# Three value loads of one sequence issued together, ahead of the next pair's keys

## The chip, the cores and the metric

The kernel runs on one core of one Trainium2 chip. The metric is the device time of one execution in microseconds, from the first to the last thing the core does. An execution under the hardware profiler gives the span, that is the time between the first and the last instruction, and the profile.

## The reference

Attention over eight sequences with eight heads feeds a two-layer block with a leaky ReLU. Sixteen "beacon" keys and values stand ahead of each sequence's own 576, and every query sees all of them.

```python
B, H, S, Nb, D = (8, 8, 576, 16, 64)
k_all = np.concatenate([beacon_k, k], axis=2)
v_all = np.concatenate([beacon_v, v], axis=2)
scores = scale * np.matmul(q, k_all.transpose(0, 1, 3, 2))
causal[:, Nb:] = np.triu(np.ones((S, S), dtype=bool), k=1)
scores = np.where(causal, -1000000000.0, scores)
scores = scores - scores.max(-1, keepdims=True)
a = np.exp(scores)
a /= a.sum(-1, keepdims=True) + 1e-09
attn_out = np.matmul(a, v_all)
...
x = np.ascontiguousarray(attn_out.transpose(0, 2, 1, 3)).reshape(B * S, H * D)
h = x @ w_in            # 4608 x 512 by 512 x 2048
g = np.maximum(0.01 * h, h)
return (g @ w_out)      # 2048 x 512
```

## The kernel before

**Units of work.** The heads are taken in pairs: pair g holds heads 2*(g % 4) and the next one of sequence g // 4, so there are 32 pairs, and pairs 8 to 11 are the third sequence (b = 2). The 592 keys and values of a sequence are cut into five parts of 128, 128, 128, 128 and 80 rows; the first part holds the 16 beacon rows. The second layer of work takes the 4608 tokens in nine chunks of 512: `up()` (L442) makes one 128-column slice of the hidden layer of a chunk, `down()` (L512 for the first chunk, L537 for the others) multiplies hidden slices with the output weights.

**Operands.** For pairs from 8 on, `load_natural` (L167, issue at L171) fetches queries (step N g.0) and keys (step N g.1) of a pair with GpSimd's DMA queue, two transfers each, one for each head. `turn_pair` (L177, L179, step T g) turns them into the operands qT and kT with two DMA transposes on SP. `load_v_cast` (L205, L209 and L214) fetches one part of a sequence's values into one of two buffers v_aug, again on GpSimd's queue; part 0 has a second small transfer for the beacon rows. GpSimd also copies the beacon columns of kT (L229, step b) and sets the masked scores to zero (`triangle`, L289). All of these stand in one order on that engine. Every transfer of GpSimd takes one of eight completion semaphores in turn, so it waits until the one eight places earlier has landed.

**Scores and values.** From pair 8 on the scores of the pairs are laid end to end and cut into tiles of 512 columns; three tiles make a block (`block`, `stretch`, L314). One pair has 1664 columns, so block 3 (columns 4608 to 6143) begins with the last 384 columns of pair 10 and goes on with pair 11. ScalarE takes the exponential (L329, L333), GpSimd masks, and `value(g, half)` (L359) multiplies with v_aug: half 0 reads parts 0 to 2 of the values, half 1 parts 0 to 4, the last part with 80 rows. VectorE divides by the sum (L388, L389), and `x_turn` (L412) turns the result by DMA for `up()`.

**What sets the order.** The whole program is written out in a manual order for all engines. The part for pairs 0 to 7 is a string of steps. It ends with "... N9.1 u b8.2 b9.2 b10.2 b11.2 x6 v7.0 T9 v7.1 d d d N10.0 N10.1 d V2.0 V2.1 x7 t0 T10", so parts 0 and 1 of the third sequence's values (V2.0, V2.1) are issued there. From pair 8 on a list of events, each with a place in time counted in pairs, is sorted and emitted; `up()` and `down()` fill the room between them. Around the change these events stand: N11.0 at 7.75, N11.1 at 8.05, block 0 at 8.6, N12.0 at 8.75, N12.1 at 9.05, T11 at 9.25, value(8, 0) at 10.25, value(8, 1) at 10.62. The loop at L805 to L807 places the remaining value loads: parts 2, 3 and 4 of sequence 2 at 8.2, 8.5 and 8.8, and the five parts of each later sequence b at 4b - 0.4, 4b - 0.1 and so on.

Of the kernel before, what the change touches and what calls it, by code (L numbers as in the profile page):

```python
# [15 lines left out]
def kernel(  # L16
# [717 lines left out]
    with order:  # L734
# [50 lines left out]
        events = []  # L785
# [18 lines left out]
                ends.append(g + 3.5)  # L804
        for b in range(2, B):  # L805
            for n in range(2 if b == 2 else 0, NKB):
                events.append((4 * b - 0.4 + 0.3 * n, 6, load_v_cast, (b, n)))  # L807
        events.sort(key=lambda e: e[:2])
        first_down[0] = 4
        w, d0 = 0, done1[0] + done2[0]  # L810
# [45 lines left out]
```

## Time and profile before

| what | us |
|---|---|
| median of 3 runs | 331.04 |
| lowest, highest | 329.14, 331.49 |
| the profiled execution | 330.95 |
| its span | 329.2 |
| PE busy (TensorE matmul) | 318.6, 97% of the span |
| ACT busy (ScalarE) | 199.8, 61% |
| POOL busy (GpSimd) | 184.7, 56% |
| DVE busy (VectorE) | 145.2, 44% |

The span was the slowest core's, and there is only one core. A row of slices in the page cuts the span into 40 equal pieces of 8.2 us; a digit is the busy share in tenths. In a timeline a line has start, duration, engine, line of the kernel, operation, what it writes and reads, and how many such instructions stand in a row; in brackets is the idle time ahead of it and what ended that. SPq marks transfers that SP issued. In a table of stretches the columns are the stretch, its length, the busy time (and count of instructions) of PE, PE's weight loads, DVE, ACT and POOL, then the granted clock of TensorE, the mean number of transfers on each DMA engine, and GB/s. Each transfer has a time to landing, from its issue until its semaphore is complete.

### The profile page before, as it was taken

Reading aid. Unit: us, or ns where it says so; the run is one execution under the profiler, and the core shown is the slowest. Engines: PE = TensorE matmul, PEld = TensorE weight load, DVE = VectorE, ACT = ScalarE, POOL = GpSimd, SP = SyncE. Lnnn points to the kernel's source line nnn. Section 1 sums busy time; section 2 is a strip of 40 time slices with the busy share of each in tenths; the row PEclk is TensorE's granted clock in tenths of the full one; section 3 lists DMA queues with packets and bytes.
Section 4 is the critical chain, followed back from the end, with each engine's and each line's share of the span. In section 5 each row is a group of like instructions: output and inputs, shape, how many; then the busy total and the mean of one; then the engine's idle time right before and its main releaser. Section 6 shows DMA issues by size and latency. Waiting matters only on the chain.

```text
span 329.2 us, 8516 instructions
## 1 busy us (share of the span) xinstructions
PE 318.6 (97%) x3429; PEld 213.1 (65%) x3429; DVE 145.2 (44%) x297; ACT 199.8 (61%) x336; POOL 184.7 (56%) x354
## 2 busy tenths in 40 slices
PE   7999999897999999999999999999999999999995
PEld 4574565443587458855788888557865684566685
DVE  3563355412565255435443444453543552424344
ACT  4968862683855885477756774786468506553510
POOL 8895978995899686658965977666221000000000
PEclk9999999997999999999999999999999999999999
DMA  8999999999999999999999999999422111000103
GB/s 134 138 203 182 145 214 124 176 154 172 130 127 165 184 126 127 143 153 110 135 137 208 126 135 127 172 106 113 110 80 58 26 53 64 2 33 32 66 32 129
DMA packets 155928, 39.93 MB, mean 121 GB/s; under 512 B 143040, under 2 KB 153152, under 8 KB 155888
## 3 DMA queue, kind: packets, MB, share of 16 engines
q0 software_dynamic: 99824, 18.54, 85.1%
q1 hardware_dynamic: 55792, 20.77, 37.2%
q8 instruction: 27, 0.44, 0.6%
q14 instruction: 13, 0.11, 0.1%
q10 hardware_dynamic: 272, 0.07, 0.1%
HBM read 37.22 MB, written 9.44 MB: 142 GB/s over the span
## 4 chain that ended last, share of the span: by engine, by line
PE 79%; POOL 6%; DMA 6%; ACT 4%; DVE 2%; issue 2%; DVEq 0%; ACTq 0%; POOLq 0%
PE acc L442 33%; PE acc L537 28%; PE av L359 8%; DMA v_aug<-in_v_dram 6%; PE sc L314 5%; ACT aT L333 3%; PE sc L267 2%; POOL v_aug L214 1%; POOL k_nat L171 1%; POOL gsum L158 1%; POOL q_nat L171 1%; DVE u L559 1%; DVE p L559 1%; PE tp L243 1%; PE acc L512 1%
## 5 line engine op out<-in xcount | busy, mean ns | idle before, releaser
L442 PE MATMUL acc<-xT,w_in_sb 128*128 128x512 bf16 (+1 forms) x640 | 137.8, 360 | 0.7 <-ACT gT L450 0.4
L450 ACT ACTIVATE gT<-acc 128x512 bf16<-128x512 f32 x144 | 83.7, 617 | 57.0 <-PE acc L442 54.5
L442 PEld LDWEIGHTS <-w_in_sb 128*128 128x128 bf16 x640 | 59.9, 98 | 53.8 <-issue 6.3
L289 POOL TENSOR_SCALAR_AFFINE_SELECT aT<-aT 128x256 bf16<-128x256 bf16 (+2 forms) x160 | 61.0, 411 | 58.3 <-ACT aT L329 34.3
L537 PEld LDWEIGHTS <-gT 128*128 128x128 bf16 x512 | 48.8, 98 | 8.3 <-issue 1.2
L333 ACT ACTIVATE aT<-sc 128x1024 bf16<-128x1024 f32 (+3 forms) x64 | 51.8, 897 | 0.0
L537 PE MATMUL acc<-w_out_sb,gT 128*128 128x256 bf16 x384 | 46.2, 273 | 0.0
L359 PEld LDWEIGHTS <-aT 128*128 128x128 bf16 (+1 forms) x960 | 36.7, 98 | 12.1 <-issue 5.9
L359 PE MATMUL av<-v_aug,aT 128*128 128x65 bf16 (+1 forms) x960 | 39.6, 194 | 4.0 <-DMA v_aug<-in_v_dram 3.1
L537 PEld LDWEIGHTS <-gsum 128*128 128x128 bf16 x384 | 36.8, 98 | 6.7
L329 ACT ACTIVATE aT<-sc 128x512 bf16<-128x512 f32 (+3 forms) x64 | 29.0, 523 | 18.6 <-PE sc L314 18.6
L562 ACT COPY p<-acc 128x512 f32<-128x512 f32 (+1 forms) x25 | 14.5, 581 | 38.8 <-PE acc L537 35.2
L388 DVE RECIPROCAL rec<-av 128x6 f32<-128x6 f32 (+1 forms) x64 | 12.0, 187 | 58.1 <-PE av L359 57.8
L214 POOL DMA_DIRECT2D v_aug<-in_v_dram x40 | 34.0, 854 | 4.0 <-DMA w_in_sb<-in_moe_w_in_dram 3.4
L171 POOL DMA_DIRECT2D k_nat<-in_k_dram x48 | 34.7, 728 | 1.9 <-issue 0.8
L171 POOL DMA_DIRECT2D q_nat<-in_q_dram x48 | 34.7, 728 | 0.3 <-issue 0.2
L389 DVE TENSOR_TENSOR x_nat<-av,rec 128x384 bf16<-128x384 f32 (+1 forms) x64 | 31.4, 491 | 2.2
L537 PE MATMUL acc<-w_sum,gsum 128*128 128x256 bf16 x256 | 31.9, 273 | 0.0
L276 ACT ACTIVATE aT<-sc 128x1024 bf16<-128x1024 f32 (+3 forms) x32 | 25.9, 875 | 4.4 <-PE sc L267 4.1
L610 DVE TENSOR_TENSOR gsum<-gT 128x1024 bf16<-128x1024 bf16 x16 | 11.0, 689 | 31.5 <-ACT gT L450 31.5
L314 PE MATMUL sc<-qT,kT 64*128 64x80 bf16 (+22 forms) x384 | 21.8, 250 | 0.6 <-PE acc L512 0.6
L314 PEld LDWEIGHTS <-kT 64*128 64x128 bf16 x384 | 12.7, 94 | 11.6 <-issue 8.0
(62 smaller groups left out, 224.5 us busy)
## 6 DMA issues: line engine op xcount, KB each, us to landing
out_dram<-p SPq DMA_DIRECT2D x26, 256.0 KB, 3.3
q_nat<-in_q_dram POOLq DMA_DIRECT2D x48, 72.0 KB, 5.4
k_nat<-in_k_dram POOLq DMA_DIRECT2D x48, 72.0 KB, 5.4
v_aug<-in_v_dram POOLq DMA_DIRECT2D x24, 128.0 KB, 6.4
w_in_sb<-in_moe_w_in_dram POOLq DMA_DIRECT2D x2, 1024.0 KB, 12.2
w_out_sb<-in_moe_w_out_dram POOLq DMA_DIRECT2D x2, 1024.0 KB, 11.0
out_dram<-u SPq DMA_DIRECT2D x8, 256.0 KB, 2.5
gsum<-in_q_dram POOLq DMA_DIRECT2D x8, 144.0 KB, 6.3
```

Of the source, the lines that this page charges most:

```text
L171: nc.gpsimd.dma_start(out=t[:, :, par], in_=(q, k)[which][b, 2 * hp + par].rearrange("(t p) d -> p t d", p=NR),)
L214: nc.gpsimd.dma_start(out=dst[lo : ROWS[c], c, :, 0:D], in_=v[b, :, OFF[c] : OFF[c] + n].rearrange("h p d -> p h d"),)
L276: nc.scalar.activation(out=aT[:, :, c0 : c0 + w], in_=sc[:, :, 0:w], func=AF.Exp, scale=0.125)
L289: nc.gpsimd.affine_select(out=view, in_=view, compare_op=ALU.is_ge, fill=0.0, base=128 - n if lo == 0 else 0, channel_multiplier=-1, patte ...
L314: nc.tensor.matmul(out=(sc[par] if apart else sc[:, par])[:, at : at + b - a], lhsT=kT[ps_, c * 128 : (c + 1) * 128], rhs=qT[ps_, q0 : q0 ...
L329: nc.scalar.activation(out=probs[g][:, par, lo:hi], in_=sc[par][:, at : at + hi - lo], func=AF.Exp, scale=0.125)
L333: nc.scalar.activation(out=probs[g][:, :, lo:hi], in_=sc[:, :, at : at + hi - lo], func=AF.Exp, scale=0.125)
L359: nc.tensor.matmul(out=avv[:, n, 0 : D + 1], lhsT=aT[0 : ROWS[c], par, a0 : a0 + 128], rhs=va[0 : ROWS[c], c, 2 * hp + par, :], start=(c = ...
L389: nc.vector.tensor_tensor(out=x_nat[:, t0:t1].rearrange("p t e d -> p (t e) d"), in0=avv[:, :, 0:D], in1=rec[:, n0:n1, None].to_broadcast( ...
L442: nc.tensor.matmul(out=acc[:, lo:hi], lhsT=w_in_cols(fc, j), rhs=xT[:, j, x0 : x0 + hi - lo], start=(j == 0), stop=(j == NJ - 1), skip_gro ...
L450: nc.scalar.activation(out=gT[i][:, fc, :], in_=acc, func=AF.Prelu, alpha=0.01)
L537: nc.tensor.matmul(out=acc[:, lo : lo + HD], lhsT=left(i, n, fc, tile), rhs=right(n, fc), start=(lo == 0 and fc == 0), stop=(fc == HF - 1) ...
```

## The change

Parts 2, 3 and 4 of sequence 2's values get one common place, 7.9, between N11.0 (7.75) and N11.1 (8.05). The later sequences' places stay as they are, written in another way.

```diff
         for b in range(2, B):
             for n in range(2 if b == 2 else 0, NKB):
-                events.append((4 * b - 0.4 + 0.3 * n, 6, load_v_cast, (b, n)))
+                events.append((4 * b - (0.1 if b == 2 else 0.4 - 0.3 * n), 6, load_v_cast, (b, n)))
```

On GpSimd's queue the order around it becomes the following, with the transfers of a step in brackets and the block's masks where they stand:

```
before: N11.0 (2)  N11.1 (2)  V2.2  V2.3  masks (4)  N12.0 (2)  V2.4  N12.1 (2)  mask ...
after:  N11.0 (2)  V2.2  V2.3  V2.4  N11.1 (2)  masks (4)  N12.0 (2)  N12.1 (2)  mask ...
```

No instruction is added or taken away on any engine, and the order on PE, VectorE, ScalarE and SP is as before. The semaphores that the transfers use are handed out in the new order.

## Prediction

> **What bounds the kernel now.** I read the page's busy rows first: PE is busy for 97% of the span, and from slice 10 on it never drops. Time can be won only where PE itself stands still, so I looked next at the two marked slices, 8 and 9 (66 to 82 us).
>
> ```profile
> PE   7999999897999999999999999999999999999995
> PEclk9999999997999999999999999999999999999999
> DMA  8999999999999999999999999999422111000103
> ```
>
> Slice 9 has a hole in PE and a dip in its granted clock; the DMA row says that the transfer engines are full there. PE's waits between 50 and 100 us name the hole, and the timeline and the chain of waits give its place:
>
> ```profile
> PE av L359 <- DMA v_aug<-in_v_dram: 2.6, 1, 2.6
> ...
> 72.65 0.90 PE L359 MATMUL av<-v_aug,aT 128*128 128x65 bf16 x24
> 76.13 0.49 PE L359 MATMUL av<-v_aug,aT 80*128 80x65 bf16 x6 [2.58 <-DMA v_aug<-in_v_dram]
> 76.43 4.06 PE L442 MATMUL acc<-xT,w_in_sb 128*128 128x512 bf16 x12
> ...
> 66.35 9.74 DMA v_aug<-in_v_dram
> 76.13 0.49 PE av L359 x6
> 76.62 3.87 PE acc L442 x12
> 80.49 0.77 PE sc L314 x16
> ```
>
> At 73.55 us PE reaches the 80-row value matmuls of pair 8, which read part 4 of the third sequence's values. That part was issued at 66.35 and landed 9.74 us later, at 76.09. PE stood for 2.58 us. The wait has a second price, in a table of four stretches:
>
> ```profile
> 72.30:75.70 3.40, 1.25 (x27) 0.92 (x26) 0.76 (x2) 1.49 (x2) 3.40 (x9) 1.00 2.33 158
> 75.70:79.10 3.40, 2.97 (x13) 1.31 (x13) 0.61 (x2) 0.60 (x1) 2.62 (x4) 0.50 2.02 154
> 79.10:82.50 3.40, 3.40 (x30) 1.48 (x29) 1.62 (x3) 2.57 (x7) 0.48 (x2) 1.00 1.91 175
> ```
>
> The column before the last two is the granted clock: 0.50 for the 3.4 us that follow the wait. The chain has twelve L442 matmuls at 3.87 us there and at 2.59 us elsewhere (82.23), so 1.28 us are lost to it.
>
> POOL issues the loads, SP the transposes that turn keys into operands:
>
> ```profile
> 60.31 1.45 POOL L171 DMA_DIRECT2D k_nat<-in_k_dram  x2
> 61.74 1.79 POOL L214 DMA_DIRECT2D v_aug<-in_v_dram  x2
> 63.50 1.48 POOL L289 TENSOR_SCALAR_AFFINE_SELECT aT<-aT 128x224 bf16<-128x224 bf16 x4
> 64.90 1.46 POOL L171 DMA_DIRECT2D q_nat<-in_q_dram  x2
> 66.35 0.73 POOL L214 DMA_DIRECT2D v_aug<-in_v_dram  x1
> 67.07 1.45 POOL L171 DMA_DIRECT2D k_nat<-in_k_dram  x2
> ...
> 65.77 1.25 SPq L179 DMA_TRANSPOSE qT<-q_nat  x1
> 67.56 1.27 SPq L179 DMA_TRANSPOSE kT<-k_nat  x1
> 68.92 0.55 SPq L522 DMA_DIRECT2D out_dram<-p  x1
> 74.99 1.20 SPq L179 DMA_TRANSPOSE qT<-q_nat  x1
> ```
>
> In POOL's rows k_nat at 60.31 is pair 11, the v_aug pair at 61.74 is parts 2 and 3, q_nat at 64.90 and k_nat at 67.07 are pair 12. In SP's rows 65.77 and 67.56 are pair 11's transposes.
>
> **What the Trainium skill says.** "TensorE: Matmul & The Clock Gate", Part 1: the array's clock is halved after an idle window of about 3.4 us, and the window runs freely. The trace agrees in the length (0.50 for 3.4 us), but a wait of 2.58 us sufficed here, in a stretch with 1.25 us of work. "DMA: Bandwidth & Descriptors", Issuing engines are not separate DMA queues: transfers of all issuers share 16 engines and interleave. The trace agrees: landings (issue plus time to landing of each transfer) come nearly in order of issue over both queues: pair 11's keys 67.1 and 67.5, part 2 at 69.5, part 3 at 71.9, pair 12's queries 72.1 and 74.8, pair 11's two transposes 74.7 and 75.9, part 4 at 76.1, pair 12's keys 77.0 and 77.3. It is one backlog, and a transfer's place in it decides. Same page, Anatomy of one DMA: waits are held on the issuing sequencer, not by the DMA engines. So SP stands at a transpose until its keys land (67.56 is 0.06 us after 67.5).
>
> **The change, part by part.** Instructions and bytes stay the same; five issues on POOL change places.
>
> Part 4's issue (0.73 us) leaves 66.35 and follows part 3. Parts 2, 3, 4 go out from 60.31: 0.91 + 0.91 + 0.73 us, so part 4 is issued at 62.1. With the longest latency of this neighbourhood, 9.9 us, it lands at 72.0; by its place in the backlog near 70 to 71. PE asks at 73.55, so the wait goes, with no doubt worth pricing. Without it PE runs 6 value matmuls (18 take 0.56, so 0.19) and 12 matmuls at full clock (2.59): 2.78 us from 73.55, against 6.94 us (73.55 to 80.49) now. PE is ready for the next block of scores at 76.3 instead of 80.5. The most that can be won is 6.94 - 2.78 = 4.16 us.
>
> The masks of pair 8 at 63.50 start 0.73 us later. Their readers start at 72.65, some 7 us after they end: free. What follows on POOL from 67.07 on stands as before, except that a load waits until the load eight places earlier has landed. Pair 13's keys (72.17, which waited 0.76 us for part 3 at 71.9) now wait for pair 11's keys. By the landing worked out next that is up to 1 us, and POOL has 3.36 us idle ahead of the masks at 82.02: free.
>
> Pair 11's keys pay. They are issued 2.55 us later, at 62.9 and 63.6, behind all three parts. In the backlog the same set as before (keys 11, parts 2 and 3) plus part 4 has to pass until the keys are in. That set was in at 71.9. Part 4 is 640 rows of 128 bytes. From 65.7 to 77.3 us 6144 such rows landed, together with the transposes and stores in between: 11.6 x 640 / 6144 = 1.2 us with everything, and about half of it, 0.6, if I count rows alone. The keys land at 72.5 to 73.1; I take 72.8 (before: 67.5). SP issues the transpose then. How long it takes isn't known: the trace has 8.3 us for this one at 67.56, 5.6 and 5.2 for pair 12's at 74.99 and 77.40, 3.6 for pair 13's at 82.66. I take 5.2, since its issue comes when the backlog ahead of it (pair 12's loads, one transpose, pair 13's queries) is being worked off; ends 3.6 and 8.3. Landing at 78.0, ends 76.4 and 81.1.
>
> Who waits for it: the block at 76.3 begins with six matmuls of pair 10 (16 take 0.77, so 0.3 us), then takes pair 11's keys at 76.6. Today they are in at 75.9, 4.8 us ahead of use. Now PE waits 78.0 - 76.6 = 1.4 us. I price no clock loss on 1.4 us: the stretch would keep 2 us of work of 3.4, more than the 1.25 that lost the clock.
>
> Behind the held transpose on SP: a store of p (68.92 becomes about 74), whose tile isn't written again before the next chunk, and pair 12's transposes at 74.99 and 77.40. Those wait for pair 12's own loads, which keep their place; SP is free at 72.8 + 1.27 + 0.55 = 74.6. They land by 82.6 as today, or sooner, and the block that needs them (86.53 today) comes at 83.7: it holds, with about 1 us to spare.
>
> Sum: 4.16 - 1.4 = 2.8 us won. The profiled execution took 330.95 us (span 329.2 and 1.7 around it), so 328.2. The median shown, 331.04, is 0.09 above the profiled execution, which changes nothing.
>
> **Rivals.** *No new wait*: the transposed keys land by 76.6. For it: the latency of 3.6 us when the backlog is short. Against: the DMA row is at 9 until slice 27. Gain 4.16, so 326.8.
>
> *The stall moves and grows* (the other side): pair 11's transpose takes its old 8.3 us, from 73.1, and lands at 81.4. PE waits 4.8 us at 76.6 and then runs 3.4 us at half clock, another 1.3 to 1.7. The loss is 6.1 to 6.5 against 4.16 won: 332.9 to 333.3. It decides from a wait of about 2.9 us with the clock lost, that is a landing at 79.5. For it: DMA is saturated, and the keys go behind all of pair 12's loads. Against: the transpose just before it in the queue is gone by then.
>
> *Nothing moves*: part 4 lands late although issued earlier. It would need over 11.4 us to landing, which no load near it took. 331.0.
>
> **How the numbers follow.** Forecast (a wait of 0.7 to 2.9 us, 327.5 to 329.7): 0.48. No new wait: 0.24. Moved and grown: 0.20. Nothing moves, or something not seen here: 0.08. The range goes from 326.6 (no new wait, with 0.2 us for the run) to 331.8, within the moved stall, of which the worst half stays out. A change of 1%, about what a measurement of this kernel can tell, is 3.3 us, a border at 327.7. Faster by more: all of "no new wait" and a fifth of the forecast, 0.34. Slower by more (over 334.3, a transpose over 9 us, or what isn't seen): 0.12. The rest, 0.54, within 1%.
>
> **What would show it.** Right: PE's waits have no v_aug entry near 73 us, the six value matmuls follow the 24 at once, and the timeline shows a PE or weight-load wait of 1 to 2 us ahead of L314 for kT near 76.6. SP shows the kT transpose of pair 11 near 73. Clock 1.00 in slice 9 says that no half-clock stretch came back. Wrong: keys in before 72, no wait at L314 (then 326.8), or a wait over 2.9 us there with the clock at 0.50 behind it.

## The result, and the profile after

The changed kernel took 328.95 us in the median of 22 executions, and the kernel before, beside it, 329.89 us in the median of 22. The ratio of the two kernels' times is 0.9979, with a 95% interval of 0.9957 to 1.0. Two further comparisons, shown below, gave 1.0002 (0.9975 to 1.0029) and 0.997 (0.9948 to 0.9993). The mean of the three is 0.9984, about 0.5 us. The forecast was 2.8 us.

The ratios leave out every execution over 1.5% longer than the fastest of its kernel, such as the profiled one of the changed kernel (span 332.5 us), which ran its first 24 us on a slower matrix clock, so that everything in it stands some 5 us later than in the profile before. I therefore count from the first score matmul of block 0 (60.30 us before, 65.53 after). The page of the changed kernel:

```profile
span 332.5 us, 8516 instructions
...
PE   8999999998999999999999999999999999999995
...
PEclk9999999999999999999999999999999999999999
DMA  8999999999999999999999999999621111000203
```

The hole of PE in slices 8 and 9 and the dip of the clock are gone. The transfers are as full as before. PE's waits between 50 and 100 us no longer name v_aug; kT has taken its place, with two waits of 0.18 and 0.97 us:

```profile
PE sc L314 <- DMA kT<-k_nat: 1.2, 2, 1.0
```

Its timeline around blocks 2 and 3 on PE, GpSimd's issues, SP's transposes, and the chain of waits at that place:

```profile
78.26 1.09 PE L359 MATMUL av<-v_aug,aT 128*128 128x65 bf16 x30
79.19 2.75 PE L442 MATMUL acc<-xT,w_in_sb 128*128 128x512 bf16 x12
81.88 0.34 PE L314 MATMUL sc<-qT,kT 64*128 64x96 bf16 x6
83.19 0.67 PE L314 MATMUL sc<-qT,kT 64*128 64x128 bf16 x10 [0.97 <-DMA kT<-k_nat]
```

```profile
66.21 2.50 POOL L214 DMA_DIRECT2D v_aug<-in_v_dram  x3
68.68 0.76 POOL L171 DMA_DIRECT2D k_nat<-in_k_dram  x1
69.75 0.73 POOL L171 DMA_DIRECT2D k_nat<-in_k_dram  x1 [0.32 <-ACT gT L450]
...
73.62 1.20 SPq L179 DMA_TRANSPOSE qT<-q_nat  x1
78.45 1.20 SPq L179 DMA_TRANSPOSE kT<-k_nat  x1
79.74 0.56 SPq L522 DMA_DIRECT2D out_dram<-p  x1
```

```profile
69.75 8.64 DMA k_nat<-in_k_dram
78.40 0.02 SPq L179
78.42 0.03 issue
78.45 4.69 DMA kT<-k_nat
83.14 0.05 issue
83.19 0.67 PE sc L314 x10
```

All 30 value matmuls follow each other (78.26). After twelve L442 matmuls PE does six score matmuls of pair 10 and then stands 0.97 us, because pair 11's keys went out behind the three values, landed at 78.39, and were turned (transposed) by 83.14. It is the new wait that the prediction describes, at the place it names. The clock was 1.00 in both stretches:

```profile
75.70:79.10 3.40, 3.23 (x46) 2.09 (x47) 0.24 (x2) 3.25 (x7) 3.40 (x9) 1.00 2.11 166
79.10:82.50 3.40, 3.12 (x26) 1.32 (x22) 1.78 (x4) 1.91 (x4) 3.40 (x8) 1.00 2.03 189
```

In this pair of profiles PE gets from the last score matmul of block 2 to the last of block 3 in 7.32 us, where before took 10.33. That is 3.0 us won, close to the 2.8 forecast. So the question is why the timed runs show a sixth of it.

### The profile page after: what moved, and what is told of

Read it like the earlier page. It is cut to its first block, busy times and chain, and to the rows that moved or that the text cites. A ratio compares the mean times of both kernels' runs of the same rounds, so it can differ in the third digit from the quotient of the medians.

```text
span 332.5 us, 8516 instructions
## 1 busy us (share of the span) xinstructions
PE 325.1 (98%) x3429; PEld 215.8 (65%) x3429; DVE 146.4 (44%) x297; ACT 201.0 (60%) x336; POOL 188.2 (57%) x354
## 4 chain that ended last, share of the span: by engine, by line
PE 81%; DMA 6%; ACT 4%; POOL 4%; DVE 2%; issue 1%; SPq 0%; DVEq 0%; ACTq 0%; POOLq 0%
PE acc L442 32%; PE acc L537 26%; PE av L359 8%; PE sc L314 5%; PE sc L267 3%; ACT aT L333 3%; PE av L645 3%; DMA k_nat<-in_k_dram 3%; PE tp L243 2%; DMA xT<-x_nat 2%; DMA kT<-k_nat 1%; POOL v_aug L214 1%; DVE u L559 1%; POOL k_nat L171 1%; DVE p L559 1%
## 5 line engine op out<-in xcount | busy, mean ns | idle before, releaser
L442 PE MATMUL acc<-xT,w_in_sb 128*128 128x512 bf16 (+1 forms) x640 | 136.6, 358 | 1.0 <-ACT gT L450 0.4
L289 POOL TENSOR_SCALAR_AFFINE_SELECT aT<-aT 128x256 bf16<-128x256 bf16 (+2 forms) x160 | 64.5, 429 | 63.2 <-ACT aT L329 29.8
L442 PEld LDWEIGHTS <-w_in_sb 128*128 128x128 bf16 x640 | 59.4, 98 | 52.9 <-issue 4.3
L333 ACT ACTIVATE aT<-sc 128x1024 bf16<-128x1024 f32 (+3 forms) x64 | 51.8, 895 | 0.0
L276 ACT ACTIVATE aT<-sc 128x1024 bf16<-128x1024 f32 (+3 forms) x32 | 26.8, 875 | 9.1 <-PE sc L267 8.6
L314 PEld LDWEIGHTS <-kT 64*128 64x128 bf16 x384 | 12.9, 94 | 12.9 <-issue 8.2
```

Source lines behind the costliest of these rows:

```text
L276: nc.scalar.activation(out=aT[:, :, c0 : c0 + w], in_=sc[:, :, 0:w], func=AF.Exp, scale=0.125)
L289: nc.gpsimd.affine_select(out=view, in_=view, compare_op=ALU.is_ge, fill=0.0, base=128 - n if lo == 0 else 0, channel_multiplier=-1, patte ...
L314: nc.tensor.matmul(out=(sc[par] if apart else sc[:, par])[:, at : at + b - a], lhsT=kT[ps_, c * 128 : (c + 1) * 128], rhs=qT[ps_, q0 : q0 ...
L333: nc.scalar.activation(out=probs[g][:, :, lo:hi], in_=sc[:, :, at : at + hi - lo], func=AF.Exp, scale=0.125)
L442: nc.tensor.matmul(out=acc[:, lo:hi], lhsT=w_in_cols(fc, j), rhs=xT[:, j, x0 : x0 + hi - lo], start=(j == 0), stop=(j == NJ - 1), skip_gro ...
```

## The experiments

There are three theories. A: the profiled execution of before is typical, and what is won at block 3 is given back later. B: the profiled execution of before was a dear one, that is, it lost more time than most, and most executions lose less at part 4. C is A's second half by itself: PE comes sooner to later operands and waits there.

To compare executions I cut PE's timeline at the last score matmul of blocks 2, 3 and 7. From block 7 to block 12 every execution in the table took 39.84 to 39.85 us (e9 alone 41.16), and from block 12 to PE's last matmul 178.93 or 178.94. So what differs lies ahead of block 7. Block 0 begins anywhere from 59.3 to 65.7 us in these profiles, and the loads that the edits move go out from about there on. From block 0 to block 2 it is 9.80 to 9.82 us, but 10.18 in the changed kernel's first profile, which has the wait of 0.18 us there, and 10.31 in e1.

| execution | block 2 to 3, us | block 3 to 7, us | sum |
|---|---|---|---|
| before, the profile of the prediction | 10.33 | 25.80 | 36.13 |
| before, e3 | 6.58 | 26.37 | 32.95 |
| before, e7 | 7.91 | 26.83 | 34.74 |
| before, e10 | 7.18 | 25.81 | 32.99 |
| changed | 7.32 | 26.52 | 33.84 |
| changed, e4 | 7.12 | 26.13 | 33.25 |
| changed, e8 | 6.49 | 26.37 | 32.86 |
| changed, e11 | 7.48 | 26.32 | 33.80 |
| part 4 alone early, e1, e12, e14 | 6.17, 6.18, 6.17 | 28.75, 27.82, 28.24 | 34.92, 34.00, 34.41 |
| value matmuls later, e9, e13, e15 | 6.35, 6.35, 6.35 | 29.27, 29.18, 26.49 | 35.62, 35.53, 32.84 |
| part 4 not loaded, e5 | 6.18 | 26.73 | 32.91 |

**The kernel before, three more profiles (e3, e7, e10).** No edit.

> The kernel before once more, for its profile. Theory A: a wait of 2.4 to 2.8 us at part 4 and a granted clock of 0.50 for 3.4 us behind it. Theory B: a wait under 2 us, or one with the clock at 1.00.

> The kernel before, a third profile. Theory B: the wait for part 4 is under 1 us and the clock stays at 1.00. Theory A: 2.4 to 2.8 us with a clock of 0.50 behind it.

> The kernel before, a fourth profile. Theory B: a wait for part 4 between 0 and 2.6 us; with a wait under 2 us no half clock.

PE's value matmuls of pair 8 in the three, in this order, from their timelines:

```profile
78.02 0.90 PE L359 MATMUL av<-v_aug,aT 128*128 128x65 bf16 x24
79.17 0.35 PE L359 MATMUL av<-v_aug,aT 80*128 80x65 bf16 x6 [0.25 <-DMA v_aug<-in_v_dram]
79.36 2.75 PE L442 MATMUL acc<-xT,w_in_sb 128*128 128x512 bf16 x12
```

```profile
74.18 0.35 PE L359 MATMUL av<-v_aug,aT 80*128 80x65 bf16 x6 [1.58 <-DMA v_aug<-in_v_dram]
74.37 2.75 PE L442 MATMUL acc<-xT,w_in_sb 128*128 128x512 bf16 x12
```

```profile
73.38 0.35 PE L359 MATMUL av<-v_aug,aT 80*128 80x65 bf16 x6 [0.85 <-DMA v_aug<-in_v_dram]
73.56 2.75 PE L442 MATMUL acc<-xT,w_in_sb 128*128 128x512 bf16 x12
```

The same wait is 0.25, 1.58 and 0.85 us long, where the profile before had 2.58. The twelve matmuls behind it take 2.75 us, where that one had 4.06: there is no half clock. For the 1.58 us wait (e7) the table of stretches says so:

```profile
72.73:76.14 3.41, 1.96 (x15) 1.01 (x15) 0.94 (x3) 0.71 (x2) 3.41 (x9) 1.00 1.93 184
76.14:79.55 3.41, 3.25 (x28) 1.52 (x28) 2.03 (x4) 2.98 (x7) 2.41 (x6) 1.00 1.98 149
```

So the wait's price, against the 6.17 us that block 2 to block 3 takes at least, was 4.16 us in the profile of the prediction and 0.41, 1.74 and 1.01 in the others. This is theory B: the profile that the sum was made on was the dearest of four, and the only one with the clock lost. B's number for e7, a wait under 1 us, was too low.

**The changed kernel, three more profiles, two of them timed (e4, e8, e11).** No edit.

> The changed kernel once more, timed beside the others. All theories: 0.4 to 1 us faster than before, as measured. Theory A further: its wait at pair 11's keys is longer than 1 us or costs the clock in most executions. Theory B: the wait is near 1 us, the clock stays at 1.00, and from the first block of scores to pair 11's scores the PE takes about 17.7 us (20.4 us in before's profile).

> The changed kernel, a third profile. Theory B: no wait for part 4, a wait for kT of 0.5 to 1.5 us at block 3, clock 1.00. If the transfers differ from execution to execution as much as the part 4 wait does (0.25 and 2.58 us so far), the wait for kT could be anywhere from 0 to 3 us.

> The changed kernel, timed once more beside before. Theory B: the ratio stays between 0.997 and 1.000, since a wait for kT of some 1 us has taken the place of a wait for part 4 of 0.25 to 2.6 us. No wait for part 4.

The ratios were 1.0002 (0.9975 to 1.0029) in e4 and 0.997 (0.9948 to 0.9993) in e11. None waited for part 4 at pair 8. Block 3 in the timelines of e4 and e11:

```profile
75.30 0.34 PE L314 MATMUL sc<-qT,kT 64*128 64x96 bf16 x6
76.42 0.67 PE L314 MATMUL sc<-qT,kT 64*128 64x128 bf16 x10 [0.77 <-DMA kT<-k_nat]
...
78.96 0.67 PE L314 MATMUL sc<-qT,kT 64*128 64x128 bf16 x10 [1.14 <-DMA kT<-k_nat]
```

In e8 the block's 16 matmuls stand in one piece of 1.16 us where they take 0.83 without a wait, so it waited 0.3 us, less than the 0.5 to 1.5 expected. The 0.4 to 1 us that e4 was expected to win did not show in its ratio. The wait for kT is thus 0.3 to 1.1 us, and steadier than what it replaces. Over four profiles each, block 2 to block 3 takes 8.0 us before (6.58 to 10.33) and 7.1 us changed (6.49 to 7.48). That is 0.9 us. Leave the dear one out and 7.2 stands against 7.1. Four profiles of each are few, so I looked at the timed executions too.

Without those that the ratios leave out, the quickest tenth of 115 executions of before took 327.9 us or less and the slowest tenth 331.3 or more; of 58 of the changed kernel it was 327.9 and 330.4. So the quick executions are alike, and the dear ones became fewer. The mean granted clock is on record for every execution, and one stretch of 3.4 us at half clock makes it 0.995. It was 0.995 or less in 21 of all 141 executions of before beside e1 to e11, and in 6 of 68 of the changed kernel. The half clock was thus rare in before, wherever in the kernel it came.

**Part 4 not loaded (e5).** This kernel leaves the load out, so its result is not the right one.

```diff
-            for n in range(2 if b == 2 else 0, NKB):
+            for n in range(2 if b == 2 else 0, NKB - 1 if b == 2 else NKB):
```

> The order of before without the load of part 4 of the third sequence's values; its 80 rows keep what the first sequence left there. Nothing waits for part 4 and nothing is moved later, and 80 KB less are fetched: more than any place for this load can give. Theory B (the wait for part 4 is short in most executions): at most 1 us faster than before, ratio 0.997 to 1.000. Theory A (it costs 4.2 us in most): 4 us faster, ratio 0.988.

The ratio was 0.9939 (0.9911 to 0.9966), 2.0 us faster (1.1 to 2.9). It lies between the two theories' numbers, so it fits neither: B had allowed at most 1 us. The value matmuls run through:

```profile
77.76 1.10 PE L359 MATMUL av<-v_aug,aT 128*128 128x65 bf16 x30
```

It agrees with the wait's mean price, 1.8 us in the four profiles of before (0.41, 1.74, 1.01 and 4.16). In its one profile nothing of that is waited for later: block 3 to block 7 takes 26.73 us. It is the only kernel here that fetches less, and the fastest; how much of its gain is owed to the smaller traffic isn't shown.

**Part 4 alone early (e1, e12, e14).** Keys of pair 11 keep their place; part 4 goes out behind parts 2 and 3, ahead of the masks.

```diff
-                events.append((4 * b - 0.4 + 0.3 * n, 6, load_v_cast, (b, n)))
+                events.append((8.55 if (b, n) == (2, 4) else 4 * b - 0.4 + 0.3 * n, 6, load_v_cast, (b, n)))
```

> Only part 4 is moved ahead, behind parts 2 and 3 and ahead of the masks; pair 11's keys keep their place ahead of the values. Theory A (the profiled execution of before was typical, so its wait plus half clock cost 4.2 us in most executions, and the keys' delay in the changed kernel takes 1.4 to 2 back): about 4 us faster than before, a ratio near 0.988. Theory B (the wait in most executions is without the half clock, or shorter; the profiled one was dear): 1 to 2.6 us faster, ratio 0.992 to 0.997, and better than the changed kernel by the keys' wait, about 1 us. Theory C (what is won here is waited for later, by transfers that come no sooner): no faster than the changed kernel. Profile: no v_aug wait near 73 us, and kT of pair 11 some 1 us later than before but ahead of use.

> The kernel with part 4 alone moved ahead, a second profile. From the last score matmul of block 2 to the last of block 3 its PE took 6.2 us, the shortest of all, but from block 3 to block 7 it took 28.8 us, where before took 25.8 to 26.8. If what part 4 no longer costs is waited for later (theory C), block 3 to block 7 takes over 27.5 us again. If the first profile's later waits were chance, 25.8 to 26.8.

> The kernel with part 4 alone moved ahead, a third profile; expected as in the second.

The ratio was 0.9987 (0.996 to 1.0013): not faster than the changed kernel, against A, and against B but for the edge of its 0.992 to 0.997. The three profiles show where the time goes. Block 2 to block 3 takes 6.17 us, without any wait. But block 3 to block 7 takes 27.8 to 28.8 us, where before and the changed kernel have 25.8 to 26.8. In e1 and then in e14 PE's timeline has:

```profile
84.50 0.61 PE L314 MATMUL sc<-qT,kT 64*128 64x512 bf16 x6 [0.61 <-DMA kT<-k_nat]
...
99.41 0.50 PE L314 MATMUL sc<-qT,kT 64*128 64x256 bf16 x6 [2.30 <-DMA kT<-k_nat]
...
83.52 0.61 PE L314 MATMUL sc<-qT,kT 64*128 64x512 bf16 x6 [0.63 <-DMA kT<-k_nat]
...
97.82 0.50 PE L314 MATMUL sc<-qT,kT 64*128 64x256 bf16 x6 [1.70 <-DMA kT<-k_nat]
```

These are the keys of pairs 12 and 14. PE comes sooner to them, but that is not all: they also come later. Turned, pair 14's keys landed 27.5 us (e1) and 27.0 us (e14) after the last score matmul of block 2, against 23.0, 24.9 and 23.1 us in e3, e7 and e10. So the sums, 34.9 and 34.4 us, are above those of e3 and e10, which did wait for part 4. Why the keys came later these runs don't show. In e12 it was xT near 109 us, for 1.48 us. Of e1's 22 timed executions 8 have a mean clock of 0.995 or less.

**Value matmuls later (e9, e13, e15).** The loads stand as before; the second value half of pair 8 goes behind the twelve L442 matmuls that followed it.

```diff
-            events.append((at + 0.37, 4, value, (g, 1)))
-            events.append((at + 0.38, 5, x_turn, (g,)))
+            later = 11.1 if g == FIRST else at + 0.37
+            events.append((later, 4, value, (g, 1)))
+            events.append((later + 0.01, 5, x_turn, (g,)))
```

> The order of loads of before; only the value matmuls of pair 8's second half are put behind the twelve L442 matmuls that follow them (2.6 us of PE), so that part 4 has 2.6 us more until it is asked for, and no key is fetched later. Theory B (part 4 comes 0.25 to 2.6 us late in before, the lost clock now and then; what the changed kernel wins there it pays at pair 11's keys): no wait for part 4 and none for kT at block 3, 1 to 2 us faster than before, ratio 0.994 to 0.997, and faster than the changed kernel. Theory C (the transfers as a whole hold PE up, and a wait removed comes back at a later operand): no faster than before, with the wait at kT or xT further on.

> The kernel with pair 8's second value half put behind twelve L442 matmuls, a second profile. Block 2 to block 3 took 6.35 us and block 3 to block 7 29.3 us in its first. Theory C: over 27.5 us again. Chance: 25.8 to 26.8.

> The kernel with pair 8's second value half later, a third profile; expected as in the second.

The ratio was 1.0014 (0.9985 to 1.0042). The wait for part 4 was gone (6.35 us from block 2 to block 3 in all three), and in two of three the time was waited for later. In e9 it was for the values and xT, with a half clock behind (its 41.16 us from block 7 to block 12), in e13 for xT:

```profile
103.38 0.35 PE L359 MATMUL av<-v_aug,aT 80*128 80x65 bf16 x6 [1.03 <-DMA v_aug<-in_v_dram]
107.36 0.38 PE L442 MATMUL acc<-xT,w_in_sb 128*128 128x512 bf16 x1 [2.11 <-DMA xT<-x_nat]
...
106.08 0.38 PE L442 MATMUL acc<-xT,w_in_sb 128*128 128x512 bf16 x1 [3.06 <-DMA xT<-x_nat]
```

Here too the operand came later: xT landed 34.6 and 34.5 us after block 2 in e9 and e13, against 32.0, 33.8 and 31.5 in e3, e7 and e10. Of these six profiles (e1, e12, e14, e9, e13, e15) five are over 27.5 us from block 3 to block 7, which is theory C's number; e15, with 26.49, is the one that waited for little. Of e9's 22 timed executions 7 have a mean clock of 0.995 or less. This edit also puts the transposes of pair 8's result behind the twelve matmuls; how much of the xT wait is owed to that wasn't tried apart. So B describes the size of the old wait, and C, in part, what these two edits met.

**Idle matmuls ahead of the wait (e2).** Order as before, PE kept active.

```diff
+            if what is value and args == (8, 1):
+                unused_ahead(8, 1, 30)
             what(*args)
```

> The order of loads of before, with 30 idle matmuls of 112 columns (about 1.5 us of PE) ahead of the value matmuls that wait for part 4. PE does nothing useful sooner, but stays active in the stretch. Theory A (the half clock after the wait is there in most executions, 1.3 us): 1.3 us faster than before, ratio 0.996. Theory B (it is there in few): the same or up to 0.5 us slower where the real wait is shorter than 1.5 us.

The ratio was 1.0037 (1.0008 to 1.0065), 1.2 us slower (0.3 to 2.1). In its profile the 30 matmuls take the place of the wait, and part 4 is there when they end:

```profile
73.68 0.53 PE L359 MATMUL av<-v_aug,aT 128*128 128x65 bf16 x12
74.05 1.64 PE L657 MATMUL av<-blank 128*128 128x112 bf16 x30
75.53 0.72 PE L359 MATMUL av<-v_aug,aT 128*128 128x65 bf16 x18
```

If the half clock came in most executions, keeping PE active would have paid. It cost most of its own 1.6 us, more than B's 0.5: that fits a wait that is mostly short, so that filling it wins little back. Its profile also waits 1.58 us for xT later (block 3 to block 7 takes 27.55 us), which may be part of the cost.

**Keys later still (e6).** The changed kernel with pair 11's keys behind the masks and pair 12's queries.

```diff
-                events.append((g - 2.95, 0, run, ("N%d.1" % g,)))
+                events.append((8.78 if g == 11 else g - 2.95, 0, run, ("N%d.1" % g,)))
```

> The changed kernel with pair 11's keys moved once more, behind the masks and pair 12's queries, so that they are issued some 4 us later than in the changed kernel and 6.5 us later than before. If the keys' landing is what PE waits for at block 3 in the changed kernel (forecast's mechanism, theory B): the wait at L314 for kT grows from 0.8 to 1.2 us to 3 to 5 us, some of the latency being made up by the shorter backlog; 2 to 5 us slower than before, ratio 1.006 to 1.015. If the changed kernel's keys had room (theory C): about as before.

The ratio was 1.0057 (1.003 to 1.0085), 1.9 us slower, just under the 2 to 5 expected. But the wait at block 3 hardly grew. It stands at 77.31 here, and the larger one in the same profile comes 23 us later, with the clock lost behind it:

```profile
77.31 0.67 PE L314 MATMUL sc<-qT,kT 64*128 64x128 bf16 x10 [1.14 <-DMA kT<-k_nat]
...
100.44 0.60 PE L314 MATMUL sc<-qT,kT 64*128 64x256 bf16 x6 [3.60 <-DMA kT<-k_nat]
...
100.70:104.10 3.40, 3.40 (x21) 2.26 (x16) 0.69 (x1) 2.00 (x3) 2.10 (x5) 0.50 1.52 172
```

The keys' transpose was issued at 74.25, 14.4 us after block 0's first matmul at 59.84 (12.9 in the changed kernel's profile), and landed in 3.0 us, not 4.7. The edit moved the keys less than the 4 us expected: they were issued 6.1 and 6.8 us after block 0's first matmul, against 3.2 and 4.2 in the changed kernel's profile. So some 2.8 us of later issue became 1.5 us of later keys and nothing at all in the turned ones: 17.4 us after block 0's first matmul, against 17.6. The expected growth at block 3 is refuted. That the loss lies at the later wait is what one profile shows; 8 of the 18 timed executions have a mean clock of 0.995 or less, so such a lost clock was common here.

## Why the prediction was right and wrong

Times of the changed kernel's profile are moved back by 5.23 us here (65.53 less 60.30), to stand beside the prediction's.

**The wait for part 4 goes: right.** It went in all four profiles. But the margin was smaller than "no doubt worth pricing": part 4 was issued at 62.7 and took 9.6 us, so it landed at 72.3, not at 70 to 71, with 1.2 us to spare ahead of 73.55. The place in the backlog gave too early a time; the bound from the longest latency of the neighbourhood, 72.0, came close.

**Pair 11's keys pay: right.** They landed at 73.2 (72.8 taken), the transpose took 4.7 us (5.2 taken) and landed at 77.9 (78.0 taken). PE waited 0.97 us (1.4 taken), since it came 0.4 us later itself, and 0.8, 0.3 and 1.1 us in the other profiles. The clock stayed at 1.00 in all four, as priced.

**The term that failed is the 4.16 us that the change could win.** It was 6.94 less 2.78 us, read from one execution and taken for all. "The median shown, 331.04, is 0.09 above the profiled execution, which changes nothing" was the step that hid it: that was the median of three. The median of 22 is 329.89, so the profiled execution, 330.95, was 1.1 us longer than the usual one. The same stretch lost 0.41, 1.74 and 1.01 us in three other executions; with the profile's own 4.16 the mean is 1.8. The half clock, 1.28 us of the 4.16, came in one of four, and somewhere in the kernel in 21 of 141 timed executions. Mean against mean at block 3, the change wins 0.9 us and not 2.8, which the measured 0.5 us fits.

**"It holds, with about 1 us to spare" for what comes behind block 3** was thought through for pair 12 alone. For the changed kernel it nearly does: block 3 to block 7 takes 26.3 us in the mean (26.1 to 26.5) against 26.2 before (25.8 to 26.8). But of the three edits that came sooner still through block 3, two lost it there, in five of six profiles; e5, which fetches less, did not. Up to block 7 the sum of the two stretches never fell below 32.8 us in any kernel; all four changed profiles stood within 1.0 us of that, and so did two of the four of before. Before's mean is 34.2 us, so some 1.4 us is what there was to win on average against the best profile of any edit here.

**The rivals.** None of the named ones describes the result. "No new wait" is refuted by the waits for kT, "moved and grown" by their length, "nothing moves" by part 4's landing ahead of use. The result's smallness lay in the price of the old wait, which no rival questioned.

What stays open is why the turned keys of pair 14 (e1, e14) and xT (e9, e13) came later than in three of the four profiles of before, and whether the 80 KB that e5 leaves out matter beyond the wait for them.

No edit tried here that computes everything is clearly faster than the changed kernel, and its own gain is small: of its three intervals one lies below 1, one reaches 1.0 and one goes beyond.

## What to carry to other kernels

A wait in a profile is one draw. Where it hangs on a transfer in a full backlog, take a few profiles of the same kernel before pricing it, and price its mean; a length of 2.6 us may stand for a wait that ranges from 0.3 to 2.6. A median of three executions doesn't show that a profile is typical. Where the transfers are full over tens of microseconds, a reordering can move the wait to the next operand that is late, and that operand can come later than before: ask what the compute engine will want next, and whether that comes sooner too. Here leaving out a transfer helped more than either way of moving the wait alone.

## What the runs showed of the hardware

Whether a wait costs the clock depended here on where it fell, and not on its length alone. In every trace the granted clock falls and rises a whole number of 3.41 us stretches after its first rise (in the profile of before it rose at 4.00 us and fell at 75.68, 21 stretches later). Cut along these stretches, the work in one decided the clock of the next, in all 17 profiles: after 1.40 us of matmul time or less the clock was halved for the next stretch, after 1.62 us or more it wasn't. The wait of 2.58 us in the profile of before left 1.29 us in its stretch and lost the clock. So did a wait of 2.11 us in e9, which lay wholly in one stretch, while one of 3.06 us in e13 lay across two and kept it. Two stretches of e9, then three of e13:

```profile
105.09:108.50 3.41, 1.30 (x19) 0.70 (x19) 1.38 (x2) 0.86 (x3) 0.00 (x0) 1.00 1.93 173
108.50:111.92 3.42, 3.20 (x9) 1.23 (x10) 0.00 (x0) 3.23 (x6) 2.21 (x6) 0.50 2.24 192
...
101.14:104.56 3.42, 1.88 (x23) 1.27 (x20) 2.39 (x5) 0.59 (x1) 2.05 (x4) 1.00 1.77 210
104.56:107.97 3.41, 1.83 (x20) 0.94 (x21) 0.00 (x0) 1.47 (x4) 0.00 (x0) 1.00 2.16 119
107.97:111.38 3.41, 3.19 (x27) 1.62 (x25) 0.75 (x2) 3.41 (x7) 2.94 (x8) 1.00 1.41 259
```

The Trainium skill's "TensorE: Matmul & The Clock Gate", Part 1, speaks of an idle window of about 3.4 us. The length agrees, but here a stretch counted as idle with up to 1.40 us of work in it.

What a later place in the backlog cost at issue came back in latency, in part or in whole. Pair 11's key transpose took 8.3 us when it was issued 7.3 us after block 0's first matmul (before), 4.7 us at 12.9 (changed) and 3.0 us at 14.4 (e6). Between the last two that made up all of the delay, between the first two only 3.7 of 5.7 us. The other profiles agree: 6.7 to 7.6 us in those of before, 4.7 to 5.2 in those of the changed kernel.
